# Whole sequences: logits ahead of their row transposes, and four scatters a pair

## The chip, the cores and the metric

The kernel runs on one core of a Trainium2 chip. A core has a matrix engine (TensorE, "PE" in the profile; its weight loads are "PEld"), a vector engine (VectorE, "DVE"), a scalar engine (ScalarE, "ACT"), GpSimd ("POOL") and a sync engine ("SP") that here only issues transfers. Each engine works through its own list of instructions in order; semaphores order the engines among each other. The metric is the device time of one execution in microseconds.

## The reference

A depthwise causal convolution over 7 positions, with softmaxed taps per head, feeds a mixture of experts with one expert per token. The expert of a token depends on the token before it: where the local gate is at least 0.5, the previous expert is kept.

```python
x = einsum('hk,bskhg->bshg', softmax(weight), windows_of_7(x))   # 8 x 3584 x 192
logits = x @ w_gate;  local = sigmoid(x @ w_local)               # 8 experts
for b in range(B):
    prev_e = -1
    for s in range(S):
        fresh_e = argmax(logits[b, s])
        e = fresh_e if s == 0 or local[b, s] < 0.5 else prev_e
        prev_e = e
        h = maximum(x[b, s] @ w1[e], 0)                          # 192 x 1024
        out[b, s] = softmax(logits[b, s])[e] * (h @ w2[e])       # 1024 x 192
```

## The kernel before

28672 tokens are worked through in 11 parts, numbered 0 to 10. Parts 0 to 5 are half sequences (1792 tokens; `SMALL` is 6). Parts 6 to 10 are whole sequences (3584 tokens, 28 tiles of 128). The diff speaks of the latter wherever it has `g >= SMALL`.

Each part from 2 on goes through these steps:

- **Convolution**, `conv` (L467). A part is held as six blocks of channels. For each, ScalarE writes the first tap into `z` (`firsts`, L481), and VectorE adds the other six (L499), so 36 steps of VectorE. There is one `z` for whole sequences, so the next part's first tap must wait until this part's `z` has been read. The loads of the following part's input (`load_chunk`, L180, on SP's queue) are issued between the steps.
- **Logits**, `logits` (L680). PE multiplies `z` with the gate weights (L707, 96 matmuls), ScalarE copies the result out of PSUM into `ls` (L712), VectorE transposes it (`lq`, L719), and sixteen small copies bring it into token order (`lt`; ScalarE at L733 for parts 6 to 9, VectorE at L735 otherwise). `rows_turned` (L687) transposes `z` into rows, one row a token, which later go to memory: four transposes of VectorE (L690). For whole sequences these four stand ahead of the logits, for half sequences behind the copies into `ls`.
- **Routing**, `route` (L741): argmax, the scan that carries the expert along, and a running count per expert give each token its place (`posi`, L888). The part's tiles are then appended to the list `to_put`.
- **Scatter**, `put` (L915). One call takes one tile of 128 tokens off `to_put` and issues on GpSimd's queue an indirect transfer of its rows to their places in `slots` (L922). With `behind`, it waits for a given matmul, so that the scatters are spread out in time.
- `tables` (L897) then fixes which expert each block of rows has.

Beside this runs the expert work, block by block, over rows that have been scattered already: 21 single blocks of 128 tokens, then pairs of 256 (blocks 21 to 58), then blocks of 512 from block 59 (`FIRST`) to 85, then pairs and singles. A pair is a hidden stage (`hidden`, L1142: 48 matmuls at L1153, four Relus of ScalarE at L1162), an output stage (`output`, L1165: 64 matmuls at L1177), and its way out: ScalarE scales one half (L1187), VectorE adds the other (L1191), GpSimd sends the rows to the output (`deliver`, L1205; the second of a pair is held back until the next hidden stage). A block of 512 takes `seven` (L1305, products at L1322, copies at L1328 to L1336) and `output_late` (L1360, matmuls at L1372). A block's rows are loaded on SP's queue (`load_rows`, L1082) and transposed by VectorE (L1134 for pairs); its expert's weights come at L1066, up to three blocks ahead. `ensure` (L1502) loads the rows of a block only once all scatters of its part have been issued.

What stands where on the engines is decided by a planner, `step` (L1432). It is called with a budget of VectorE time: for a pair 3.9 after the hidden stage, 1.2 after the output stage, ahead of L1191, and 3.3 at the end. It spends the budget on `conv` or `route`, whose `yield`s give the cost of what they just issued: 1.15 for a step of the convolution of a whole sequence, 0.24 times 7 tiles, 1.68, for each of the four row transposes. What is overspent is taken off the next budget. Three words are yielded beside costs:

- `"pe"` ends the route's turn; its logits are issued when the planner is called the next time (in blocks of 512, the next time at one place of a later block).
- `"hop"` lets the next part's convolution start, if it may (`st["turned"]`), and gives it the rest of the budget.
- `"placed"` does nothing.

The scatters of a pair are issued in `output`, behind the matmuls named in `spots`: at three places, or at five while more than 14 tiles wait (`len(to_put) > NT`). `spots` maps a place to the number of tiles that must be left in the list for it to be used.

Of the kernel before, what the change touches and what calls it, by code (L numbers as in the profile page):

```python
# [24 lines left out]
NT = 14  # L25
# [106 lines left out]
def kernel(  # L132
# [372 lines left out]
    def wide_route(g, y_sb, lt):  # L505
# [91 lines left out]
        nc.vector.tensor_copy(posi, pos)  # L597
        nc.vector.tensor_tensor(y[:, :, 0], pr, rs, op=Alu.mult)
        for b in range(NB):
            to_put.append((HALF if g and b < NH else g, y[:, b, :], posi[:, b:b + 1]))  # L600
        yield
        if g == 0:
            first_table(upto[:, :, NB], pos)
# [76 lines left out]
    def logits(g, z):  # L680

        nt = NTS[g]
        tq = (nt + 3) // 4
        y_sbs = row_tiles(g)
        zt = z.rearrange("p b (t s) -> p t b s", s=Q)

        def rows_turned():  # L687
            for t in range(0, nt, tq):
                u = min(t + tq, nt)
                nc.vector.transpose(y_sbs[t // NT][:, t % NT:t % NT + u - t, Y0:Y0 + D]  # L690
                                    .rearrange("p t (b s) -> p t b s", s=Q), zt[:, t:u])
                yield 0.24 * (u - t)

        if g >= SMALL:
            yield from rows_turned()
        yield "pe"
        if late_p or st["block"] >= TURNED:
            both = (st["bank"].tile([P, 2, 512], F32, name="ps") if late_p
                    else xps_p.tile([P, 2, 512], F32, name="xps"))
            lps = [both[:, half, :tq * Q] for half in range(2)]  # L700
        else:
            lps = [hps_p.tile([P, tq * Q], F32, name="hps") for half in range(2)]
        begin = [min(tq * j, nt - tq) for j in range(4)]
        for b in range(DQ):
            for j in range(4):
                for half, rows in halves():
                    nc.tensor.matmul(lps[half][Q * j:Q * j + Q, :], lhsT=wgq[rows, b, :],  # L707
                                     rhs=z[rows, b, begin[j] * Q:(begin[j] + tq) * Q],
                                     start=(b == 0), stop=(b == DQ - 1))
        ls = tmp(g, "ls", [P, 2, tq * Q], bufs=1)  # L710
        for half in range(2):
            nc.scalar.copy(ls[:, half, :], lps[half])  # L712
        if g < SMALL:
            yield from rows_turned()
        st["turned"] = g
        if g >= SMALL:
            yield "hop"
        lq = tmp(g, "lq", [P, 2 * tq, Q], bufs=1)
        nc.vector.transpose(lq.rearrange("p t e -> p (t e)"), ls.rearrange("p h x -> p (h x)"))  # L719
        yield 0.4  # L720
        lt = tmp(g, "lt", [P, nt, E + 1])
        aside = SMALL <= g < LAST
        if aside and late_p:
            yield "hop"
        for r in range(4):
            for j in range(4):
                t, u = tq * j, min(tq * (j + 1), nt)
                at = r // 2 * tq + t - begin[j]
                e0 = r % 2 * (E + 1)
                dst = lt[Q * r:Q * r + Q, t:u, :]  # L730
                src = lq[Q * j:Q * j + Q, at:at + u - t, e0:e0 + E + 1]
                if aside:
                    nc.scalar.copy(dst, src)  # L733
                else:
                    nc.vector.tensor_copy(dst, src)  # L735
                    yield 0.12
            if aside and r % 2:
                yield "hop"
        return y_sbs, lt

    def route(g):  # L741
# [145 lines left out]
        posi = sm.tile([P, nt], I32, name="posi", bufs=3)  # L887
        nc.vector.tensor_copy(posi, pos)  # L888
        for t in range(nt):
            to_put.append((g, y_sbs[t // NT][:, t % NT, :], posi[:, t:t + 1]))  # L890
        yield 0.2
        nc.vector.tensor_tensor(base, base, nps[:, 1, :E], op=Alu.add)
        yield 0.2
# [21 lines left out]
    def put(behind=None):  # L915


        if not to_put:
            return
        g, rows, to = to_put.pop(0)  # L920
        nc.gpsimd.nop()
        ins = nc.gpsimd.indirect_dma_start(  # L922
            out=slots[:, :], in_=rows, in_offset=None,
            out_offset=bass.IndirectOffsetOnAxis(ap=to, axis=0)).ins
        if behind is not None:
            tc.add_manual_dep(ins, behind.ins.name, SYNC, reason="scatters apart")
        if puts:
            tc.declare_no_dep(ins, group="puts", reason="slots of their own")
        if g:
            tc.declare_no_dep(ins, group="gets", reason="those slots were full before")  # L930
        puts.append((g, ins))
        tc.add_to_no_dep_group("puts", ins)
        tc.add_to_no_dep_group(f"puts{g}", ins)
# [73 lines left out]
    def fill(g):  # L1007


        lim = sm.tile([P, E], F32, name="lim")  # L1010
        nc.vector.tensor_scalar(lim, used, float(UT), None, Alu.mult)
        yield 0.2
        to = sm.tile([P, E], F32, name="to")
        nc.vector.tensor_scalar(to, base, i_of, None, Alu.add)
        yield 0.2
        over = sm.tile([P, E], F32, name="over")
        nc.vector.tensor_tensor(over, to, lim, op=Alu.is_ge)
        yield 0.2
        nc.vector.tensor_tensor(to, to, ec, op=Alu.add)
        yield 0.2  # L1020
        nc.vector.tensor_scalar(to, to, 1.0, None, Alu.add)
        yield 0.2
        far = sm.tile([P, E], F32, name="far")
        nc.vector.scalar_tensor_tensor(far, ef, float(UT), to, Alu.mult, Alu.subtract)
        yield 0.2
        nc.vector.tensor_scalar(far, far, float((DUMMY + 1) * UT), None, Alu.add)
        yield 0.2
        nc.vector.scalar_tensor_tensor(far, far, i_of, over, Alu.add, Alu.mult)
        yield 0.2
        nc.vector.tensor_tensor(to, to, far, op=Alu.add)  # L1030
        yield 0.2
        toi = sm.tile([P, E], I32, name="toi")
        nc.vector.tensor_copy(toi, to)
        yield 0.2
        for e in range(E):
            to_put.append((PADS, pad, toi[:, e:e + 1]))


    blocks = [(0, 1, i, next(g for g in FULL if i < FULL[g])) for i in range(ONE[-1])]
# [102 lines left out]
    def hidden(n, wb, xT, w1):  # L1142
# [4 lines left out]
        for two in range(2):  # L1147
            hps = [hps_p.tile([P, 2, BT], F32, name="hps") for half in range(2)]
            for d in range(KD):
                for j in range(2):  # L1150
                    f0 = (d * 4 + two * 2 + j) * P
                    for half, rows in halves():
                        ins = nc.tensor.matmul(hps[half][:, j, w], lhsT=wb[rows, w1 + f0:w1 + f0 + P],  # L1153
                                               rhs=xT[rows, d, w], start=(d == 0 and j == 0),
                                               stop=(d == KD - 1), skip_group_check=True)
                if two and d == 0 and held:
                    held.pop(0)(ins)
                if n == 1 and (two, d) == (0, 0) and st["block"] and not (st["hot"] or few()):
                    put(ins)
            for half in range(2):  # L1160
# [4 lines left out]
    def output(n, wb, xg, hT, w2):  # L1165
# [2 lines left out]
        away = st["due"] and not (to_put and to_put[0][0] == 3)  # L1168
        spots = {1: {(0, 0, 1): 0} if st["block"] and not away else {},
                 2: {(0, 0, 0): 0, (0, 1, 1): 2, (2, 0, 7): 0}}[n]  # L1170
        if to_put and (to_put[0][0] in (HALF, 3) or n > 1 and len(to_put) > NT):
            spots.update({1: {(2, 0, 3): 0}, 2: {(2, 0, 2): 0, (2, 1, 6): 0}}[n])
        for m4 in ([0, 1, 4, 5], [2, 3, 6, 7]):
            for k in range(n):
# [568 lines left out]
```

## Time and profile before

| | us |
|---|---|
| median of three runs | 1308.93 (1304.45 to 1313.44) |
| profiled execution | 1307.49 |
| its span, first to last instruction | 1305.6 |

The timeline lists an engine's instructions as start, duration, engine, line, operation, what it writes and reads, and how many of the same kind were merged (x2). What stands in brackets is how long the engine had been idle before it, and what ended that. "issue" means that nothing the profile shows was waited for. The ends of matmuls are modelled. The page gives, for each engine, its busy time, its share of the span, and the number of its instructions; the row "DMA" is the busy share of the transfer engines in 40 equal slices, in tenths; the chain is the work that ended last, followed back from the end.

Pairs run from about 180 us to 614 us of the span, blocks of 512 from there to about 1170 us.

### The profile page before, as it was taken

What the parts mean: (1) busy time and instruction counts of PE and PEld (TensorE: products, weight loads), DVE (VectorE), ACT (ScalarE), POOL (GpSimd) and SP (SyncE); (2) the same over time, 40 slices, a digit from 0 to 9 for tenths busy, and PEclk for the clock granted to TensorE, in tenths of its full rate; (3) what the DMA queues carried; (4) which work ended last, traced back from release to release, by engine and by line L of the source; (5) the groups of instructions that cost most, each with busy time, mean ns of one, the idle gap of its engine ahead of it and who ended that gap; (6) DMA issues with size and microseconds to landing.
All of it is one profiled execution on the core that took longest, in us unless ns stands there. A gap on an engine that the chain in (4) does not pass through costs nothing.

```text
span 1305.6 us, 37317 instructions
## 1 busy us (share of the span) xinstructions
PE 1265.1 (97%) x14674; PEld 1216.0 (93%) x14674; DVE 878.0 (67%) x1951; ACT 524.7 (40%) x1039; POOL 589.4 (45%) x636
## 2 busy tenths in 40 slices
PE   9899999999999999999999999999999999999997
PEld 8799989999988889889999998999999999999997
DVE  6889778989787787787869889578544435421111
ACT  5455533334243333424445444353434434432232
POOL 4544451536226446447633567435666433321111
PEclk9999999999999999999999999999999999999999
DMA  5899898959858869768755636274655544546794
GB/s 198 275 412 345 346 343 247 299 169 354 293 158 275 272 179 323 253 211 248 204 158 133 178 119 201 83 189 144 168 173 142 167 142 118 156 124 211 233 330 148
DMA packets 187784, 284.61 MB, mean 218 GB/s; under 512 B 150352, under 2 KB 160775, under 8 KB 174162
## 3 DMA queue, kind: packets, MB, share of 16 engines
q1 hardware_dynamic: 165280, 236.94, 57.8%
q0 software_dynamic: 22320, 45.22, 10.3%
q8 instruction: 117, 1.92, 0.6%
q14 instruction: 65, 0.53, 0.1%
q10 hardware_dynamic: 2, 0.00, 0.0%
HBM read 236.50 MB, written 46.07 MB: 216 GB/s over the span
## 4 chain that ended last, share of the span: by engine, by line
PE 89%; DVE 5%; issue 2%; DMA 1%; ACT 1%; POOL 0%; another core or an unknown queue 0%; SPq 0%; POOLq 0%; DVEq 0%; ACTq 0%
PE ps L1372 24%; PE yps L1177 20%; PE hps L1153 19%; PE ps L1322 14%; PE ps L1267 5%; PE xps L1322 3%; DVE arena L499 2%; DMA hT<-slots 1%; PE xps L707 1%; PE hps L281 1%; DMA wb<-in_w_dram 0%; PE ps L707 0%; DVE xT L1246 0%; PE hps L218 0%; DVE hot L662 0%
## 5 line engine op out<-in xcount | busy, mean ns | idle before, releaser
L1205 POOL DMA_INDIRECT out_dram<-o_sb,head x208 | 230.5, 1108 | 468.9 <-DVE o_sb L1387 289.7
L1372 PE MATMUL ps<-wb,hot 64*128 64x192 f32 x4224 | 354.0, 323 | 1.1 <-issue 0.7
L1372 PEld LDWEIGHTS ps<-wb,hot 64*128 64x128 f32 x4224 | 343.9, 187 | 6.6 <-issue 3.8
L499 DVE SCALAR_TENSOR_TENSOR arena<-arena,c 128x896 f32<-128x896 f32 (+1 forms) x324 | 305.2, 951 | 38.0 <-ACT arena L481 30.9
L922 POOL DMA_INDIRECT slots<-arena,posi x228 | 236.8, 1039 | 162.0 <-PE yps L1177 82.8
L1177 PE MATMUL yps<-wb,hT 64*128 64x192 f32 x3104 | 279.9, 331 | 11.7 <-ACT hT L1162 7.6
L1153 PE MATMUL hps<-xT,wb 64*128 64x256 f32 (+1 forms) x2832 | 279.7, 342 | 7.1 <-issue 6.5
L1177 PEld LDWEIGHTS yps<-wb,hT 64*128 64x128 f32 x3104 | 267.5, 192 | 17.7 <-ACT hT L1162 9.8
L1153 PEld LDWEIGHTS hps<-xT,wb 64*128 64x128 f32 x2832 | 250.3, 188 | 25.9 <-issue 13.0
L1162 ACT ACTIVATE hT<-hps 128x512 f32<-128x512 f32 (+1 forms) x236 | 110.1, 520 | 157.9 <-PE hps L1153 120.4
L1387 DVE SCALAR_TENSOR_TENSOR o_sb<-ps,head,o_sb 128x192 f32<-128x192 f32 x132 | 49.5, 412 | 155.3 <-ACT o_sb L1382 154.3
L1382 ACT ACTIVATE o_sb<-ps,head 128x192 f32<-128x192 f32 x132 | 49.1, 418 | 233.8 <-PE ps L1372 223.0
L1322 PE MATMUL ps<-xT,wb 64*128 64x256 f32 x864 | 104.2, 376 | 0.5 <-DVE xT L1298 0.5
L1322 PEld LDWEIGHTS ps<-xT,wb 64*128 64x128 f32 x864 | 91.8, 187 | 1.2 <-issue 0.9
L1187 ACT ACTIVATE o_sb<-yps,head 128x192 f32<-128x192 f32 x76 | 27.9, 418 | 152.5 <-PE yps L1177 127.5
L1343 DVE TENSOR_TENSOR hot<-xps,hot 128x512 f32<-128x512 f32 x54 | 37.0, 685 | 62.0 <-PE xps L1322 61.6
L1267 PE MATMUL ps<-xT,wb 64*128 64x128 f32 (+1 forms) x912 | 66.7, 299 | 0.0
L1267 PEld LDWEIGHTS ps<-xT,wb 64*128 64x128 f32 x912 | 65.1, 188 | 0.0
L1344 ACT ACTIVATE hot<-hot 128x512 f32<-128x512 f32 x54 | 34.1, 632 | 74.9 <-DVE hot L1343 62.7
L1322 PE MATMUL ps<-xg 64*128 64x256 f32 x432 | 58.0, 380 | 2.9 <-issue 1.0
L1191 DVE SCALAR_TENSOR_TENSOR o_sb<-yps,head,o_sb 128x192 f32<-128x192 f32 x76 | 28.1, 411 | 40.1 <-ACT o_sb L1187 24.8
L1246 DVE STREAM_TRANSPOSE xT<-arena 128x768 f32<-128x768 f32 (+1 forms) x37 | 31.7, 887 | 33.0 <-PE ps L1267 21.8
(308 smaller groups left out, 1340.3 us busy)
## 6 DMA issues: line engine op xcount, KB each, us to landing
wb<-in_w_dram SPq DMA_DIRECT2D x101, 1536.0 KB
arena<-in_xl_dram SPq DMA_DIRECT2D x30, 544.0 KB
hot<-slots SPq DMA_DIRECT2D x152, 96.0 KB
arena<-slots SPq DMA_DIRECT2D x56, 192.0 KB
hT<-slots SPq DMA_DIRECT2D x52, 192.0 KB
arena<-in_x_dram SPq DMA_DIRECT2D x4, 1920.0 KB
wb<-in_w_dram SPq DMA_DIRECT2D x12, 512.0 KB
slots<-arena,posi POOLq DMA_INDIRECT x228
```

Source lines behind the costliest of these rows:

```text
L499: nc.vector.scalar_tensor_tensor(z[:, b, :], chans(b, k), c[:, b, k:k + 1], z[:, b, :], Alu.mult, Alu.add)
L922: ins = nc.gpsimd.indirect_dma_start(out=slots[:, :], in_=rows, in_offset=None, out_offset=bass.IndirectOffsetOnAxis(ap=to, axis=0)).ins
L1153: ins = nc.tensor.matmul(hps[half][:, j, w], lhsT=wb[rows, w1 + f0:w1 + f0 + P], rhs=xT[rows, d, w], start=(d == 0 and j == 0), stop=(d == ...
L1162: nc.scalar.activation(hT[:, m:m + 2, w], hps[half][:, :, w], Act.Relu)
L1177: ins = nc.tensor.matmul(yps[half][:, k * D:(k + 1) * D], lhsT=hT[rows, m, k * P:(k + 1) * P], rhs=wb[rows, w2 + m * D:w2 + (m + 1) * D], ...
L1205: sent = nc.gpsimd.indirect_dma_start(out=out, in_=o, in_offset=None, out_offset=bass.IndirectOffsetOnAxis(ap=xg.bitcast(I32)[:, k, 1:2], ...
L1267: nc.tensor.matmul(hps[:, half, j, :], lhsT=wb[rows, f0:f0 + P], rhs=xT[rows, d, :], start=(d == 0 and j == 0), stop=(d == KD - 1), skip_g ...
L1322: ins = nc.tensor.matmul(to[:, half, j, :], lhsT=b[rows, j * P:(j + 1) * P], rhs=a[rows, :], start=(first and j == 0), stop=True, skip_gro ...
L1343: nc.vector.tensor_tensor(h11[:, side], wbk[:, side], h11[:, side], op=Alu.add)
L1372: ins = nc.tensor.matmul(yps[:, half, k * D:(k + 1) * D], lhsT=h[two][rows, side, j, k * P:(k + 1) * P], rhs=wb[rows, f * D:(f + 1) * D], ...
L1382: nc.scalar.activation(o_sb[:, k, :], yps[:, 0, k * D:(k + 1) * D], Act.Copy, scale=xg[:, at + k, 0:1])
L1387: nc.vector.scalar_tensor_tensor(o_sb[:, k, :], yps[:, 1, k * D:(k + 1) * D], xg[:, at + k, 0:1], o_sb[:, k, :], Alu.mult, Alu.add)
```

## The change

It does four things.

1. For parts 6 to 10, the row transposes are issued behind the logits and the copies into `ls`, as for the smaller parts. The `"hop"` behind them is gone.
2. Each entry of `to_put` also holds the number of the block in which its position was computed (-1 for the first two parts and for padding). A `put` that is tied to a matmul does nothing if the entry at the head of the list was computed in the current block. This holds until block 59; from there on the rule is off (`late_p` is set).
3. The pair's hidden stage gets a scatter, behind the second of the three groups of matmuls of its first half (`(two, d) == (0, 1)`), for parts 6 and up.
4. The two extra places in a pair's output stage are left to part 3 (and to the half part); the rule "more than 14 wait" is gone. So a pair has four scatters for whole sequences, and three for half sequences.

```diff
@@ wide_route, parts 0 and 1
-            to_put.append((HALF if g and b < NH else g, y[:, b, :], posi[:, b:b + 1]))
+            to_put.append((HALF if g and b < NH else g, y[:, b, :], posi[:, b:b + 1], -1))
@@ logits
-        if g >= SMALL:
-            yield from rows_turned()
         yield "pe"
...
         for half in range(2):
             nc.scalar.copy(ls[:, half, :], lps[half])
-        if g < SMALL:
-            yield from rows_turned()
+        yield from rows_turned()
         st["turned"] = g
-        if g >= SMALL:
-            yield "hop"
@@ route
-            to_put.append((g, y_sbs[t // NT][:, t % NT, :], posi[:, t:t + 1]))
+            to_put.append((g, y_sbs[t // NT][:, t % NT, :], posi[:, t:t + 1], st["block"]))
@@ put
-        if not to_put:
+        if not to_put or behind is not None and not late_p and to_put[0][3] == st["block"]:
             return
-        g, rows, to = to_put.pop(0)
+        g, rows, to, _ = to_put.pop(0)
@@ fill
-            to_put.append((PADS, pad, toi[:, e:e + 1]))
+            to_put.append((PADS, pad, toi[:, e:e + 1], -1))
@@ hidden
+                if n == 2 and (two, d) == (0, 1) and to_put and to_put[0][0] >= SMALL:
+                    put(ins)
@@ output
-        if to_put and (to_put[0][0] in (HALF, 3) or n > 1 and len(to_put) > NT):
+        if to_put and to_put[0][0] in (HALF, 3):
             spots.update({1: {(2, 0, 3): 0}, 2: {(2, 0, 2): 0, (2, 1, 6): 0}}[n])
```

## The prediction

> **What bounds the kernel now.** Read in this order: the page (busy shares, slices, chain), then the timeline of ScalarE cut to line 1187, then the timelines of the odd pairs.
>
> ```profile
> PE 1265.1 (97%) x14674; PEld 1216.0 (93%) x14674; DVE 878.0 (67%) x1951; ACT 524.7 (40%) x1039; POOL 589.4 (45%) x636
> ...
> DMA  5899898959858869768755636274655544546794
> ...
> PE 89%; DVE 5%; issue 2%; DMA 1%; ACT 1%; POOL 0%; another core or an unknown queue 0%; SPq 0%; POOLq 0%; DVEq 0%; ACTq 0%
> ```
>
> PE bounds it: 89% of the chain. A change to planning and scatters can only win the places where PE loses time, so I look for these. L1187 empties a pair's result as soon as PE has it, so the distance between two of its starts is what a pair took.
>
> ```profile
> 341.55 0.73 ACT L1187 ACTIVATE o_sb<-yps,head 128x192 f32<-128x192 f32 x2 [4.18 <-PE yps L1177]
> 351.93 0.73 ACT L1187 ACTIVATE o_sb<-yps,head 128x192 f32<-128x192 f32 x2 [4.18 <-PE yps L1177]
> 369.83 0.73 ACT L1187 ACTIVATE o_sb<-yps,head 128x192 f32<-128x192 f32 x2 [2.65 <-PE yps L1177]
> 380.21 0.73 ACT L1187 ACTIVATE o_sb<-yps,head 128x192 f32<-128x192 f32 x2 [3.84 <-PE yps L1177]
> ...
> 426.14 0.73 ACT L1187 ACTIVATE o_sb<-yps,head 128x192 f32<-128x192 f32 x2 [3.23 <-PE yps L1177]
> ...
> 446.90 0.73 ACT L1187 ACTIVATE o_sb<-yps,head 128x192 f32<-128x192 f32 x2 [4.11 <-PE yps L1177]
> 462.76 0.73 ACT L1187 ACTIVATE o_sb<-yps,head 128x192 f32<-128x192 f32 x2 [0.96 <-PE yps L1177]
> 473.14 0.73 ACT L1187 ACTIVATE o_sb<-yps,head 128x192 f32<-128x192 f32 x2 [3.84 <-PE yps L1177]
> ...
> 519.63 0.73 ACT L1187 ACTIVATE o_sb<-yps,head 128x192 f32<-128x192 f32 x2 [4.12 <-PE yps L1177]
> ...
> 540.39 0.73 ACT L1187 ACTIVATE o_sb<-yps,head 128x192 f32<-128x192 f32 x2 [4.12 <-issue]
> 557.95 0.73 ACT L1187 ACTIVATE o_sb<-yps,head 128x192 f32<-128x192 f32 x2 [2.65 <-PE yps L1177]
> ...
> 578.71 0.73 ACT L1187 ACTIVATE o_sb<-yps,head 128x192 f32<-128x192 f32 x2 [4.12 <-PE yps L1177]
> ...
> 614.55 0.73 ACT L1187 ACTIVATE o_sb<-yps,head 128x192 f32<-128x192 f32 x2 [4.11 <-PE yps L1177]
> ```
>
> These are the ends of blocks 35, 36, 37, 38, 42, 44, 45, 46, 50, 52, 53, 55 and 58. An undisturbed pair takes 351.93 - 341.55 = 10.38 us. Two sorts of places take longer. (a) The pairs ahead of which a whole sequence's logits run: 17.90, 15.86 and 17.56 us (parts 6, 7, 8). (b) The pairs just after a part's positions were computed: blocks 39 to 42 took 45.93 us, 4.41 over four pairs; 47 to 50 took 46.49, 4.97 over; 56 to 58 took 35.84, 4.70 over three. Together (b) is 14.1 us.
>
> Sort (a), from the timeline of part 6:
>
> ```profile
> 352.13 2.50 PE L707 MATMUL xps<-arena,wg 64*32 64x224 f32 x96
> 355.22 1.98 ACT L481 ACTIVATE arena<-arena,c 128x896 f32<-128x896 f32 x2
> 356.31 2.34 DVE L499 SCALAR_TENSOR_TENSOR arena<-arena,c 128x896 f32<-128x896 f32 x2 [8.29 <-ACT arena L481]
> 359.22 0.64 DVE L719 STREAM_TRANSPOSE arena<-arena 128x448 f32<-128x448 f32 x1
> 359.94 2.04 ACT L733 COPY arena<-arena 32x63 f32<-32x63 f32 x8 [2.74 <-DVE arena L719]
> 362.00 2.06 ACT L1162 ACTIVATE hT<-hps 128x512 f32<-128x512 f32 x4
> 362.65 7.15 PE L1177 MATMUL yps<-wb,hT 64*128 64x192 f32 x64 [2.64 <-ACT hT L1162]
> ...
> 457.26 4.98 PE L1177 MATMUL yps<-wb,hT 64*128 64x192 f32 x58 [2.58 <-ACT hT L1162]
> ```
>
> The logits cost PE 2.50 and that stays. But the eight copies of L733 stand on ScalarE ahead of the Relu L1162 that PE waits for; they wait for L719, which stands on VectorE behind L499, which waits for L481, which waits for the logits. VectorE sits idle 8.29 us and PE 2.64, and PE's next 64 matmuls then take 7.15, where half a pair, 5.19, is usual. So (a) is 17.90 - 12.88 = 5.02, 2.98 and 4.68: 12.7 us. After much the same gap, 2.58, part 7's matmuls did not slow (4.98 for 58), so the slow-down is a matter of chance. [...]
>
> **The change, part by part.** *Logits first.* The planner spends 3.9, 1.2 and 3.3 on a pair, 1.15 for a tap and four times 1.68 for the row transposes. In block 35 the 3.9 ends with the last tap of part 6; the 1.2 starts the route, which now says "pe" at once, and the 3.3 emits the logits. They move from the end of block 36 to the end of block 35, likewise 44 to 43, 52 to 51, and in the late blocks 61 to 60 and 69 to 68. The four transposes, L719 and the copies follow in block 36. Their rows:
>
> ```profile
> 340.16 1.58 DVE L690 STREAM_TRANSPOSE arena<-arena 128x1344 f32<-128x1344 f32 x1
> 342.66 3.03 DVE L690 STREAM_TRANSPOSE arena<-arena 128x1344 f32<-128x1344 f32 x2
> 345.61 0.94 DVE L1134 STREAM_TRANSPOSE xT<-hot 128x768 f32<-128x768 f32 x1
> ...
> 437.22 1.58 DVE L690 STREAM_TRANSPOSE arena<-arena 128x1344 f32<-128x1344 f32 x1
> ```
>
> From the end T of block 35's output (341.5) VectorE does L1191 to T+1.2, two transposes to 4.2, L1134 to 5.2, two more to 8.2, L719 to 8.9; ScalarE copies to 10.9 and runs the next part's two first taps (L481) to 12.9. PE has logits to 2.5, hidden stage to 7.7, output to 12.9. Both Relus of block 36 are ahead of the copies on ScalarE, and L1187 is due at 12.9, so nothing stands before PE; the second eight copies run from 13.6 to 15.7 while PE's next half hidden stage ends at 15.5. Gain: 12.7. Cover: if L1134 is late by over 2 us (its rows not landed), L1187 is late by the excess, and PE needs its banks at T+18.
>
> What is late next: z, the convolved part, itself. Formerly the transposes hid it. Part 6's z was ready at 340.16, before PE came (341.5). Part 7's was ready at 437.22, when block 43's output had ended 0.7 before (10.38 before 446.90, so 436.52). I charge 0.7 for parts 7 and 8 each, 1.4; the bounds are 0 and 1.4. Next taps start on VectorE some 3 us after L719, idle time that costs PE nothing. SP's chunk loads, issued with the taps, move half a block earlier past that pair's scatters only.
>
> *Late blocks.* Part 9's logits come a block earlier. Their old cost and the new one:
>
> ```profile
> 680.03 2.00 PE L1322 MATMUL ps<-xT,wb 64*128 64x256 f32 x16 [0.53 <-DVE xT L1298]
> ...
> 687.91 1.13 PE L1322 MATMUL ps<-xT,xg 64*128 64x256 f32 x8 [0.69 <-DVE hot L1346]
> ```
> ```profile
> 656.98 1.01 ACT L1328 COPY hot<-ps 128x1024 f32<-128x1024 f32 x1 [0.18 <-PE ps L1322]
> 658.38 1.09 PE L1322 MATMUL ps<-xg 64*128 64x256 f32 x8
> ```
>
> Old waits 0.53 + 0.69 = 1.2 go. New: eight copies (2.04) and one first tap (0.99) are emitted in block 61's last step, ahead of L1328 of block 62, which PE needs 0.39 after its end: 2.04 + 0.99 - 0.39 = 2.6 lost (0 if the banks hide it; 4.6 with a slow stretch of 1.95 behind it). Part 10's copies are VectorE's and stay hidden.
>
> *Scatters.* Positions come half a block earlier (end of 38 for 39, and so on). 28 scatters go four a pair, one of them in the hidden stage, where there were five and then three. POOL gains no work: at 1.27 us apart, four and two deliveries take 7.6 of 10.38. The new one stands ahead of the held delivery; that result buffer is wanted two blocks on. Part 5's scatters start a block later, so SP loads block 38's rows with block 39's; weights queued behind them are wanted three blocks on. Sort (b), from block 39:
>
> ```profile
> 387.93 0.18 DVE L888 CAST posi<-pos 128x28 int32<-128x28 f32 x1
> ...
> 388.88 0.97 POOL L922 DMA_INDIRECT slots<-arena,posi  x1 [3.98 <-PE yps L1177]
> ...
> 391.68 0.35 SPq L1066 DMA_DIRECT2D wb<-in_w_dram  x1
> ...
> 393.96 1.83 POOL L922 DMA_INDIRECT slots<-arena,posi  x1 [0.30 <-issue]
> ...
> 395.32 0.49 PE L1153 MATMUL hps<-xT,wb 64*128 64x256 f32 x2 [0.26 <-issue]
> ```
> ```profile
> 278.49 0.73 ACT L1187 ACTIVATE o_sb<-yps,head 128x192 f32<-128x192 f32 x2 [3.93 <-PE yps L1177]
> ...
> 300.03 0.73 ACT L1187 ACTIVATE o_sb<-yps,head 128x192 f32<-128x192 f32 x2 [3.25 <-issue]
> ```
>
> The positions come after the matmuls behind which the block's scatters were put, so five go out back to back, with the next weights (391.68) beside them, and PE falters in the next hidden stage for no releaser shown. Part 5, with three scatters in such a run, lost only 300.03 - 278.49 - 20.76 = 0.78. The new run: positions came 387.93 - 380.21 = 7.7 into block 39 and now come a 3.3 step earlier, at about 4.5; the four scatters and the held delivery behind them take 6.4 and end at 10.9, ahead of the next weights (391.68 - 380.21 = 11.5). No row shows such a run, so the gain lies between nothing (below it, see the rival) and 14.1; I take part 5's 0.78 for each of the three as nearest: 14.1 - 2.3 = 11.8 won, and 0.8 at part 5, whose run goes.
>
> Sum against the profiled execution's 1307.49 (span 1305.6, 1.9 around it): -12.7 +1.4 -1.2 +2.6 -11.8 -0.8 = -22.5, so 1285.0. The median of the runs shown, 1308.93, is 1.4 higher: **1286.5**.
>
> **The rivals.** *The faltering stays:* it comes from the weights and chunks, which keep their place, not from the scatters. For it: no releaser is shown. Against: it follows each such run and no ordinary pair. Then 1286.5 + 11.8 = **1298**. [...]
>
> *It only moves:* if VectorE is some 3 us later than counted, PE waits as long for z, or for banks behind a late L1187, as it did for the Relu, and the scatters meet the weights after all. Then 12.7 and 11.8 are not won, the 1.4 being part of it: 1286.5 + 24.5 - 1.4 = **1310**. Against: the slack counted above.
>
> *Slower:* the scatter in the hidden stage makes PE falter there, in each of the 20 pairs that get one (39 to 58). At 0.78 each that is 15.6 over 1298, **1314**; from 1.2 us each it is over 1% slower (1322). For it: all faltering was in a hidden stage. Against: pairs with three spaced scatters ran at 10.38.
>
> **How the numbers follow.** A measurement of this kernel tells about 1% from no change, 13 us. Forecast 0.56, faltering stays 0.25, moves 0.11, slower 0.08. Faster: 0.54 of the first and 0.03 of the second, 0.57; slower 0.08; within 1% the rest, 0.35. The range reaches from all of 14.1 won, no wait for z and no loss at block 62 (1286.5 - 2.3 - 1.4 - 2.6 = 1280, less a us of scatter) to the second case with slow stretches behind two new gaps (1298 + 3.9, 1302); likeliest case alone: 1279 to 1292.
>
> **What would show it.** Right: L1187 distances of 12.9 to 13.6 where the logits run, no idle 8.29 on VectorE, L733 ended before L1187 is due; 10.38 to 10.6 in the pairs after the positions; a wait of L1322 on ScalarE at block 62's start. Wrong: PE waiting on L499 at L707, matmuls with "issue" gaps in hidden stages, or SP's row loads landing after L1134 wants them.

## The result and the profile after

The changed kernel took 1288.55 us, the median of four runs (1286.63 to 1289.84), beside 1309.97 for the kernel before on the same chips. The ratio is 0.9839, with a 95% interval of 0.9801 to 0.9877: 1.6% faster. The prediction was 1286.5 (1279 to 1302). The profiled execution took 1289.84, its span is 1288.0.

Of the page of the changed kernel: busy time of the engines and shares of the chain of waits.

```profile
PE 1255.7 (97%) x14674; PEld 1207.1 (94%) x14674; DVE 879.3 (68%) x1951; ACT 523.8 (41%) x1039; POOL 593.6 (46%) x636
...
PE 93%; DVE 4%; issue 1%; ACT 1%; POOL 0%; another core or an unknown queue 0%; POOLq 0%; DVEq 0%; ACTq 0%
```

PE still bounds the kernel, with more of the chain (93% after 89%) and less "issue" (1% after 2%). The work is the same, the losses are fewer. Lines of the changed kernel carry smaller numbers: L1187 is now L1184, L707 is L705, L1177 is L1174, L733 is L728, L922 is L917, L1191 is L1188, L1205 is L1202, L1298 is L1295, L1322 is L1319, L1328 is L1325.

The timeline of ScalarE cut to L1184, the end of each pair's output. The rows are those of blocks 35, 36, 38, 42, 43, 44, 51, 52 and 58.

```profile
343.65 0.73 ACT L1184 ACTIVATE o_sb<-yps,head 128x192 f32<-128x192 f32 x2 [4.12 <-PE yps L1174]
357.65 0.73 ACT L1184 ACTIVATE o_sb<-yps,head 128x192 f32<-128x192 f32 x2 [0.21 <-PE yps L1174]
...
378.41 0.73 ACT L1184 ACTIVATE o_sb<-yps,head 128x192 f32<-128x192 f32 x2 [4.12 <-PE yps L1174]
...
419.93 0.73 ACT L1184 ACTIVATE o_sb<-yps,head 128x192 f32<-128x192 f32 x2 [4.12 <-PE yps L1174]
430.31 0.73 ACT L1184 ACTIVATE o_sb<-yps,head 128x192 f32<-128x192 f32 x2 [4.12 <-issue]
444.33 0.73 ACT L1184 ACTIVATE o_sb<-yps,head 128x192 f32<-128x192 f32 x2 [0.22 <-PE yps L1174]
...
516.99 0.73 ACT L1184 ACTIVATE o_sb<-yps,head 128x192 f32<-128x192 f32 x2 [4.12 <-issue]
531.05 0.73 ACT L1184 ACTIVATE o_sb<-yps,head 128x192 f32<-128x192 f32 x2 [0.22 <-PE yps L1174]
...
593.54 0.73 ACT L1184 ACTIVATE o_sb<-yps,head 128x192 f32<-128x192 f32 x2 [4.28 <-PE yps L1174]
```

The pairs with logits are now 36, 44 and 52, and take 14.00, 14.02 and 14.06 us instead of 17.90, 15.86 and 17.56. Blocks 39 to 42 take 419.93 - 378.41 = 41.52, four times the undisturbed 10.38: PE no longer falters behind the positions. From the end of block 35 to that of block 58 stand 23 pairs and three logits, 23 x 10.38 + 3 x 2.50 = 246.2 us without a loss. The kernel before took 614.55 - 341.55 = 273.0 there, the new one 593.54 - 343.65 = 249.9. So it lost 26.8 us in this stretch and now loses 3.7. This number, the **loss of the stretch**, is used for all kernels below. The rest of the 3.7 beside the logits is 0.2, in blocks 53 and 58.

The timeline around the logits of part 6:

```profile
343.55 1.99 PEld L705 LDWEIGHTS xps<-arena,wg 64*32 64x32 f32 x78 [0.23 <-issue]
343.55 3.49 PE L705 MATMUL xps<-arena,wg 64*32 64x224 f32 x96
...
344.77 3.03 DVE L690 STREAM_TRANSPOSE arena<-arena 128x1344 f32<-128x1344 f32 x2
344.80 0.98 POOL L1202 DMA_INDIRECT out_dram<-o_sb,head  x1 [1.23 <-DVE o_sb L1188]
...
346.10 0.51 PEld L705 LDWEIGHTS xps<-arena,wg 64*32 64x32 f32 x18 [0.56 <-issue]
...
353.42 2.01 ACT L728 COPY arena<-arena 32x63 f32<-32x63 f32 x8
355.46 1.98 ACT L481 ACTIVATE arena<-arena,c 128x896 f32<-128x896 f32 x2
...
356.54 2.34 DVE L499 SCALAR_TENSOR_TENSOR arena<-arena,c 128x896 f32<-128x896 f32 x2 [4.44 <-ACT arena L481]
```

The logits start on time, with nothing from L499 to wait for. The copies L728 and the two first taps L481 end at 357.44, just ahead of L1184 at 357.65. But the logits themselves take 3.49 us, where they took 2.50, with a gap of 0.56 in their weight loads. That is about 1.0 in each of three parts, most of what is left of the 3.7.

### The profile page after: what moved, and what is told of

Read it like the earlier page. It is cut to its first block, busy times and chain, and to the rows that moved or that the text cites. A ratio compares the mean times of both kernels' runs of the same rounds, so it can differ in the third digit from the quotient of the medians.

```text
span 1288.0 us, 37312 instructions
## 1 busy us (share of the span) xinstructions
PE 1255.7 (97%) x14674; PEld 1207.1 (94%) x14674; DVE 879.3 (68%) x1951; ACT 523.8 (41%) x1039; POOL 593.6 (46%) x636
## 4 chain that ended last, share of the span: by engine, by line
PE 93%; DVE 4%; issue 1%; ACT 1%; POOL 0%; another core or an unknown queue 0%; POOLq 0%; DVEq 0%; ACTq 0%
PE ps L1369 25%; PE hps L1148 20%; PE yps L1174 20%; PE ps L1319 16%; PE ps L1264 5%; PE xps L1319 3%; PE xps L705 1%; DVE arena L499 1%; PE hps L281 1%; PE ps L705 1%; PE hps L218 0%; DVE hot L662 0%; PE hps L705 0%; PE yps L668 0%
## 5 line engine op out<-in xcount | busy, mean ns | idle before, releaser
L1202 POOL DMA_INDIRECT out_dram<-o_sb,head x208 | 220.9, 1062 | 458.3 <-DVE o_sb L1384 298.5
L499 DVE SCALAR_TENSOR_TENSOR arena<-arena,c 128x896 f32<-128x896 f32 (+1 forms) x324 | 305.1, 951 | 24.9 <-ACT arena L481 17.6
L917 POOL DMA_INDIRECT slots<-arena,posi x228 | 251.8, 1104 | 145.7 <-PE yps L1174 66.0
L1148 PE MATMUL hps<-xT,wb 64*128 64x256 f32 (+1 forms) x2832 | 273.3, 341 | 4.2 <-issue 3.9
L1174 PE MATMUL yps<-wb,hT 64*128 64x192 f32 x3104 | 273.3, 326 | 3.2 <-ACT hT L1159 2.5
L1174 PEld LDWEIGHTS yps<-wb,hT 64*128 64x128 f32 x3104 | 261.2, 188 | 7.5 <-ACT hT L1159 3.7
L1148 PEld LDWEIGHTS hps<-xT,wb 64*128 64x128 f32 x2832 | 246.4, 188 | 21.5 <-issue 8.1
L1319 PE MATMUL ps<-xT,wb 64*128 64x256 f32 x864 | 104.5, 376 | 2.6 <-DVE xT L1295 2.6
L1319 PEld LDWEIGHTS ps<-xT,wb 64*128 64x128 f32 x864 | 91.6, 187 | 3.8 <-issue 3.4
L1184 ACT ACTIVATE o_sb<-yps,head 128x192 f32<-128x192 f32 x76 | 27.8, 417 | 128.3 <-PE yps L1174 105.1
L1319 PE MATMUL ps<-xg 64*128 64x256 f32 x432 | 57.7, 380 | 6.5 <-POOL xg L1285 3.0
L1319 PEld LDWEIGHTS ps<-xg 64*128 64x128 f32 x432 | 45.3, 187 | 9.9 <-POOL xg L1285 3.7
```

Source lines behind the costliest of these rows:

```text
L499: nc.vector.scalar_tensor_tensor(z[:, b, :], chans(b, k), c[:, b, k:k + 1], z[:, b, :], Alu.mult, Alu.add)
L917: ins = nc.gpsimd.indirect_dma_start(out=slots[:, :], in_=rows, in_offset=None, out_offset=bass.IndirectOffsetOnAxis(ap=to, axis=0)).ins
L1174: ins = nc.tensor.matmul(yps[half][:, k * D:(k + 1) * D], lhsT=hT[rows, m, k * P:(k + 1) * P], rhs=wb[rows, w2 + m * D:w2 + (m + 1) * D], ...
L1202: sent = nc.gpsimd.indirect_dma_start(out=out, in_=o, in_offset=None, out_offset=bass.IndirectOffsetOnAxis(ap=xg.bitcast(I32)[:, k, 1:2], ...
L1319: ins = nc.tensor.matmul(to[:, half, j, :], lhsT=b[rows, j * P:(j + 1) * P], rhs=a[rows, :], start=(first and j == 0), stop=True, skip_gro ...
```

## The experiments

All are judged by the ratio to the kernel before on the same chip, and by the loss of the stretch in their own profiles (last row of block 58 less that of block 35, less 246.2).

| kernel | ratio, 95% interval | loss of the stretch, us |
|---|---|---|
| before | 1 | 26.8 |
| whole change | 0.9839 (0.9801 to 0.9877) | 3.7 |
| whole change, again (c1) | 0.985 (0.9829 to 0.9871) | 3.5 |
| e1 part 1 alone | 0.983 (0.9808 to 0.9851) | 6.5 |
| e2 parts 2 to 4 | 0.9905 (0.9884 to 0.9926) | 13.9 |
| e3 part 2 alone | 0.9958 (0.9934 to 0.9983) | 19.0 |
| e4 other order of products | 0.9815 (0.9794 to 0.9837) | 3.6 |
| e5 delivery held back | 0.9815 (0.9791 to 0.9838) | 1.3 |
| e5b the same, again | 0.9812 (0.9787 to 0.9838) | 1.3 |
| e6 run of four, output stage | 0.9888 (0.9862 to 0.9913) | 8.4 |
| e7 run of four, hidden stage | 0.9977 (0.996 to 0.9995) | 23.3 |
| e8 the same with pauses | 0.9883 (0.9851 to 0.9916) | 13.2 |
| e9 e5 and late blocks | 0.9807 (0.9777 to 0.9836) | 1.3 |
| e10 e1 with delivery held back | 0.9835 (0.9805 to 0.9865) | 5.4 |

The loss of the stretch comes from one profile a row, but it repeats: 3.7 and 3.5 for the whole change, 1.3 and 1.3 for e5.

### Which part did it

**e1**, the kernel before with part 1 alone:

```diff
-        if g >= SMALL:
-            yield from rows_turned()
         yield "pe"
...
-        if g < SMALL:
-            yield from rows_turned()
+        yield from rows_turned()
         st["turned"] = g
-        if g >= SMALL:
-            yield "hop"
```

> Part 1 of the change alone: logits ahead of the row transposes; the scatters by the old rule (five a pair while more than 14 wait, no block left out). The positions then come at the end of block 38, so the five scatters of block 39 find them there and go out spread over the output stage. Theory R (PE falters only behind a run of scatters that goes out back to back because the positions came late): both sorts of loss go, 10.38 us in the pairs after the positions, about 1289 us, as with the whole change. Theory D (five scatters a pair beside the weight loads are the cause, however they are spread): blocks 39 to 42, 47 to 50 and 56 to 58 still take some 14 us more than their 10.38 each, about 1302 us.

Measured: 0.983, the same as the whole change within the interval; loss 6.5. The timeline of ScalarE of this kernel, the ends of blocks 38 and 43:

```profile
378.62 0.73 ACT L1182 ACTIVATE o_sb<-yps,head 128x192 f32<-128x192 f32 x2 [4.11 <-PE yps L1172]
...
431.00 0.73 ACT L1182 ACTIVATE o_sb<-yps,head 128x192 f32<-128x192 f32 x2 [4.15 <-issue]
```

Five scatters a pair are still issued, but these five pairs take 431.00 - 378.62 = 52.4 us, 0.5 over; the three places together lost 2.8 instead of 14.1. The part that moves the logits also removed most of the faltering: the positions came half a block earlier, so the scatters found them ready and went out where they were put. Theory D, by which five scatters a pair lose some 14 us however they are spread, fell.

**e2**, the changed kernel with part 1 undone (the reverse of the diff above):

> Parts 2 to 4 alone: four scatters a pair, none in the block in which its position was computed; logits behind the row transposes as before. The pairs with logits still take 17.9, 15.9 and 17.6 us, the late blocks their old time. Theory R: the late positions of block 39 start no run, the scatters begin spread in block 40, no faltering: 1310 - 14 = 1296 us. Rival (the faltering went because the positions came half a block earlier): it stays, 1308 to 1310 us.

Measured: 0.9905. The pairs with logits took 15.91, 15.86 and 18.31, in all 50.1 where the kernel before took 51.3. That is 11.4 over, so of the loss of 13.9 the faltering behind the positions has 2.5 us, where it had 14.1: nearly as far as theory R had it. The rival, by which it goes only with earlier positions, fell.

**e3**, the kernel before with the rule of part 2 alone:

```diff
...
-        if not to_put:
+        if not to_put or behind is not None and not late_p and to_put[0][3] == st["block"]:
             return
...
```

> Part 2 alone: no scatter in the block in which its position was computed; otherwise as before, five a pair. Theory R: no run, faltering gone, 1296 us. Theory D (five a pair): it stays, 1308 to 1310 us. The pairs with logits as before, 17.9, 15.9 and 17.6 us.

Neither: 0.9958, and a loss behind the positions of 8.3 us instead of 14.1. The run behind block 39 is gone, but a new one formed behind block 41 (four scatters and a delivery, 1.26 apart, from 411.85 on), since five a pair stand close together in the output stage. So theory R has to be put in terms of spacing, not of late positions.

**e10**, part 1 with the delivery held back (the edit of e5 below), beside e5b, which has parts 2 to 4 as well:

> Part 1 of the change with the delivery held back, without parts 2 to 4. In the run of part 1 alone the pairs behind the positions lost 2.8 us against 0.2 with the whole change. If parts 2 to 4 are worth that, this is 2.6 us above the control, 0.9835 of the kernel before; if they are worth nothing, the same as the control.

0.9835 beside 0.9812: the intervals overlap, so the runs don't tell them apart. The traces do: a loss of 5.4 beside 1.3, and 6.5 (e1) beside 3.6 (e4) without the held delivery. Parts 2 to 4 are worth 3 to 4 us, 0.3%, once part 1 is in.

### What makes PE falter

**e6 and e7** put the four scatters of a pair at one place:

```diff
-                if n == 2 and (two, d) == (0, 1) and to_put and to_put[0][0] >= SMALL:
-                    put(ins)
...
+        run = n == 2 and to_put and to_put[0][0] >= SMALL
+        if run:
+            spots = {(0, 0, 0): 0}
...
-                        put(ins)
+                        for _ in range(4 if run else 1):
+                            put(ins)
```

> The whole change, but the four scatters of a pair for whole sequences are issued at one place, behind the first matmuls of the output stage, one right after the other; none in the hidden stage. Their number and blocks are the same. At that place the loads that SP issued at the pair's start have mostly landed. Theory R (a run of scatters is enough): the 20 pairs that carry them lose PE time, at part 5's 0.78 each some 16 us. Theory RD (it takes a run beside the loads of weights, rows and chunks): about the time of the whole change, within 4 us.

e7 has the same loop, in the hidden stage, and no spots in the output stage:

> The whole change, but the four scatters of a pair for whole sequences are issued at one place, behind the second group of matmuls of the hidden stage, one right after the other; none in the output stage. There SP's loads of weights, rows and chunks are under way. Theory R and theory RD: the 20 pairs lose PE time, 0.78 to 4.7 each, 16 to 90 us in all. Rival (runs do not matter, only that the positions were late): the time of the whole change.

e6 lost 8.4 (4.7 more than the change), e7 lost 23.3. So neither place is free, as the rival to theories R and RD had it; but the 16 us that theory R put for e6 did not come either. The two don't tell the place from the length of a run: in e6 GpSimd often idled some 2 us behind the four scatters, while in blocks 39 and 47 of e7 they stood in runs of six. The timelines of GpSimd and of PE's weight loads in block 39 of e7:

```profile
380.99 0.99 POOL L1205 DMA_INDIRECT out_dram<-o_sb,head  x1 [7.34 <-DVE o_sb L1191]
382.28 0.97 POOL L917 DMA_INDIRECT slots<-arena,posi  x1 [0.30 <-issue]
383.56 0.96 POOL L917 DMA_INDIRECT slots<-arena,posi  x1 [0.31 <-issue]
384.82 0.96 POOL L917 DMA_INDIRECT slots<-arena,posi  x1 [0.30 <-issue]
386.08 0.96 POOL L917 DMA_INDIRECT slots<-arena,posi  x1 [0.30 <-issue]
386.70 0.21 PEld L1177 LDWEIGHTS yps<-wb,hT 64*128 64x128 f32 x2 [0.72 <-issue]
387.35 1.80 POOL L1205 DMA_INDIRECT out_dram<-o_sb,head  x1 [0.30 <-issue]
388.12 0.20 PEld L1177 LDWEIGHTS yps<-wb,hT 64*128 64x128 f32 x2 [1.21 <-issue]
```

Six transfers start 1.27 us apart. Five microseconds after the first, PE's weight loads stop for 0.72 us, go on for two loads, and stop for 1.21, and pair 39 takes 14.98. In pair 40 of the same kernel as many scatters stand at the same place, and it takes 10.38:

```profile
395.27 3.53 DVE L499 SCALAR_TENSOR_TENSOR arena<-arena,c 128x896 f32<-128x896 f32 x3
395.31 0.99 POOL L1205 DMA_INDIRECT out_dram<-o_sb,head  x1 [6.16 <-DVE o_sb L1191]
396.60 1.86 POOL L917 DMA_INDIRECT slots<-arena,posi  x1 [0.30 <-issue]
398.76 0.96 POOL L917 DMA_INDIRECT slots<-arena,posi  x1 [0.30 <-issue]
398.93 5.41 PEld L1177 LDWEIGHTS yps<-wb,hT 64*128 64x128 f32 x64
399.62 4.56 DVE L499 SCALAR_TENSOR_TENSOR arena<-arena,c 128x896 f32<-128x896 f32 x4
400.03 1.53 POOL L917 DMA_INDIRECT slots<-arena,posi  x1 [0.30 <-issue]
401.87 0.96 POOL L917 DMA_INDIRECT slots<-arena,posi  x1 [0.30 <-issue]
403.13 1.90 POOL L1205 DMA_INDIRECT out_dram<-o_sb,head  x1 [0.30 <-issue]
```

Here half of the transfers take 1.5 to 1.9 us, beside taps of VectorE (L499), the starts lie 1.3 to 2.2 apart (1.56 in the mean), and the 64 weight loads run through. The pairs of the kernel before (180 to 614 us) show the same: of 52 transfers with no tap beside them the longest took 1.02 us, while of 129 with one 37 took over 1.3 and up to 1.91. Not every transfer beside a tap is long: those at 395.31 and 401.87 took 0.99 and 0.96. Why some are is not shown. Behind the positions VectorE fixes the tables, in steps of at most 0.34 us beside one transpose of 0.98, and the first five transfers of block 39 took 0.96 to 0.99 there; this fits the place of the loss.

**e8** puts a short work of GpSimd behind each scatter of e7:

```diff
                     for _ in range(4):
                         put(ins)
+                        nc.gpsimd.memset(sm.tile([P, 256], F32, name="pause", bufs=1), 0.0)
```

> The run of four scatters in the hidden stage once more, with a memset of GpSimd (128 x 256) behind each of them, so that the transfers are issued some 1.6 us apart or more instead of 1.27. Their number, their place and the loads beside them are the same. In the run without pauses the pairs 39, 47, 53 and 55 lost 4.6, 4.4, 3.6 and 2.3 us; in 39 and 47 six transfers went out 1.27 apart; in pairs 40 to 42 the same scatters went out 1.6 to 2.2 apart, slowed by VectorE's taps, and PE lost 0 to 0.2. Theory RR (the spacing decides): pairs 39 and 47 lose less than 1 us each, the whole is some 12 us below the run without pauses, about 0.988 of the kernel before. Rival (the number of transfers beside the loads decides): no change, 0.998 of the kernel before.

The timeline of GpSimd in block 39 of this kernel:

```profile
382.07 0.97 POOL L917 DMA_INDIRECT slots<-arena,posi  x1 [0.30 <-issue]
383.03 0.33 POOL L1156 MEMSET pause<- 128x256 f32 x1
383.54 0.97 POOL L917 DMA_INDIRECT slots<-arena,posi  x1 [0.17 <-issue]
```

The pause gave a spacing of 1.46 instead of 1.27, less than was meant. Pair 39 took 12.62 instead of 14.98, pair 47 11.91 instead of 14.78. Theory RR had asked for a loss under 1 us in each; they lost 2.2 and 1.5. The whole is 0.9883 beside 0.9977, with intervals apart: the 12 us that were expected. The rival, no change, fell. A fifth of a microsecond more between transfers halves the loss of these pairs, with the number of transfers, their place and the loads unchanged. Outside the pairs with logits the loss of the stretch went from 18.5 to 6.8. In two pairs with logits it grew (44 and 52: 15.38 and 15.67 beside 14.52 and 14.87), for a reason given in the next section. That the spacing of GpSimd's transfers counts is shown; that nothing else contributes is not.

### What keeps the logits at 3.5 us

**c1** is the changed kernel again, as a control.

> The whole change once more, as the control for the three others of this set on the same chip: 0.984 times the kernel before.

**e4** begins the products with the block of channels that VectorE finishes last, so that PE's wait for it moves from the 41st of 48 pairs of products to the first:

```diff
-        for b in range(DQ):
+        for n, b in enumerate([DQ - 1] + list(range(DQ - 1)) if g >= SMALL else range(DQ)):
...
-                                     start=(b == 0), stop=(b == DQ - 1))
+                                     start=(n == 0), stop=(n == DQ - 1))
```

> The whole change, with the gate products of whole sequences starting at the last block of channels, the one that is convolved last; the sum over the blocks is taken in another order. In the changed kernel PE waits for VectorE at the 41st of 48 pairs of products, and L705 takes 3.4 us where it took 2.5. Theory W (the wait in the middle, though met, makes the gap of 0.56 and the rest): with the wait at the first product L705 takes 2.5 again in parts 6 to 8, 3 x 0.9 less, about 1286 us. Rival (the gap comes from elsewhere, as it does in parts 9 and 10, which have no such wait): L705 stays at 3.4, 1288.5 us.

The pairs took 14.03, 14.02 and 14.05, the gap stayed: theory W fell. What all logits with a gap had in common was a transfer that GpSimd issued beside them. So it was in the kernel before, where part 10's logits alone took 3.44 us instead of 2.50 (timeline of the kernel before):

```profile
841.25 1.26 POOL L1205 DMA_INDIRECT out_dram<-o_sb,head  x1 [4.82 <-DVE o_sb L1387]
...
842.53 0.17 PEld L707 LDWEIGHTS ps<-arena,wg 64*32 64x32 f32 x5 [0.56 <-issue]
```

**e5** (and e5b, the same on another chip) holds that delivery back:

```diff
-                if two and d == 0 and held:
+                if two and d == 0 and held or not two and d == 2 and len(held) > 1:
                     held.pop(0)(ins)
...
-            if k == 0 and not st["hot"]:
+            if k == 0 and not st["hot"] and not (n > 1 and st["due"] and st["block"] >= TURNED):
                 deliver(o_sb[:, 0, :], xg, 0)
```

> The whole change; in the pairs behind which logits are issued, the delivery that follows L1188 at once is held back as well, until the third group of matmuls of the next hidden stage. So no transfer of GpSimd is issued beside the gate products. In the runs so far each of eight logits beside which such a transfer was issued had a gap of about 0.56 in its weight loads and took 3.4 us, and each of nine without one had no gap and took 2.5 us. Theory P (the transfer that GpSimd issues makes the gap): L705 takes 2.5 us in parts 6 to 8, the three pairs 13.1 instead of 14.0, 2.8 us less than the whole change. Rival Q (the row transposes of VectorE that now run beside the products make it): L705 stays at 3.4 us, no change.

> The version that holds the delivery back while logits run, once more as the control for the next two on the same chip: 0.9815 of the kernel before.

The timeline of e5 around part 7's logits:

```profile
430.19 2.07 PEld L705 LDWEIGHTS xps<-arena,wg 64*32 64x32 f32 x96 [0.23 <-issue]
...
431.40 3.03 DVE L690 STREAM_TRANSPOSE arena<-arena 128x1344 f32<-128x1344 f32 x2
...
436.16 0.99 POOL L1202 DMA_INDIRECT out_dram<-o_sb,head  x1 [0.30 <-issue]
```

All 96 weight loads run through in 2.07, in parts 6, 7 and 8 alike, with the row transposes still beside them. Theory P holds, rival Q falls. All 14 profiles agree, by number too: of their 70 logits of whole sequences, the 25 with no such transfer beside them took 2.50 or 2.51, the 41 with one 3.2 to 3.6 (beside the 3.60 of e1's part 8 a second one ended 0.1 us into them), and the 4 with two 4.3 to 4.4 (parts 7 and 8 of e6 and e8; this is why pairs 44 and 52 of e8 grew). Nor does the amount of data moved decide it: in the kernel before, part 6 had no gap while the transfer engines moved 207 GB/s (352.1 to 354.6 us), and part 10 had one at 18 GB/s (839.7 to 843.2). The median was 1287.36 (1283.0 to 1289.12) beside 1290.92 (1289.8 to 1292.45) for the control on the same chip, 3.6 less; the loss of the stretch fell from 3.5 to 1.3.

### The late blocks

**e9** adds two edits to e5: while late logits run, their block's first delivery is held back too, and the second eight copies of part 9 are issued one place later.

```diff
+                due = st["due"]
                 step(SIDE[2 + part], late_p[0] if part == 0 else None)
+                due = due and not st["due"]
...
-                if k == 0 or n < KQ:
+                if (k == 0 or n < KQ) and not (n == KQ and due):
...
-            if n == KQ and part and two == 0 and k and held:
+            if n == KQ and part and two == 0 and held and (k or len(held) > 1):
                 held.pop(0)(ins)
...
             if aside and r % 2:
                 yield "hop"
+                if late_p and r == 1:
+                    yield "hop"
```

> The same, and two edits in the late blocks: the delivery is held back there too while logits run, and the second eight copies of part 9's logits are issued one place later, so that L1325 of block 62 does not stand behind them. Expected: no gap of 0.56 in the logits of parts 9 and 10 (2 x 0.9), and L1325 of block 62 free of the copies' 2.0, with PE's wait of 1.11 gone: 2.9 us less than the control, 0.979 of the kernel before. Rival (the copies only delay L1341 and VectorE's first steps of the routing instead): 1.8 less or nothing.

The timeline of e9 (its L1327 is L1325 of the changed kernel):

```profile
630.61 2.07 PEld L705 LDWEIGHTS ps<-arena,wg 64*32 64x32 f32 x96 [0.23 <-issue]
...
660.21 1.01 ACT L1327 COPY hot<-ps 128x1024 f32<-128x1024 f32 x1
...
664.43 2.02 ACT L728 COPY arena<-arena 32x63 f32<-32x63 f32 x8
```

The gap in part 9's logits is gone (part 10's too), the copies stand behind L1327 instead of ahead of it, and PE's wait of 1.11 in block 62 is gone with them. The wait of 0.91 ahead of it stayed. From the end of block 58 to L1327 of block 64 it took 107.2 us, where e5b took 109.0. The median was 1288.49 beside 1291.09, 2.6 less, with ratios of 0.9807 and 0.9812: what the traces show, though the runs alone don't separate the two.

## Why the prediction was right

Both mechanisms held, and most of the time came where it was forecast. That the sum came so close is in part luck: the logits won 2.1 us less than forecast and the faltering 2.1 more, and the late blocks and the start of the span each cost 2 to 3 us that the sum did not have.

**The logits (forecast: 12.7 won, 1.4 lost to z).** The three pairs took 51.32 before and 42.08 after: 9.2 were won. The mechanism was right: no Relu waited for the copies any more, and VectorE's idle 8.29 is down to 4.44. The 1.4 did not come: VectorE's last tap of part 7 ended at 428.9, 1.3 before PE started the logits at 430.2. In its place came about 1.0 for each of three logits, 3.49 instead of 2.50 in part 6, which the prediction had carried over unchanged ("that stays"). It had counted the delivery of L1202 among GpSimd's work only, not as something that slows PE. Before, no transfer stood beside these logits.

**The slow clock.** The prediction counted the row of 7.15, behind a gap of 2.64, as a slow stretch and a matter of chance. The granted clock bears this out: it was 0.50 there from 365 to 367 us. The changed kernel has no gap of 2.6 there, but e3 has them. The timeline of its PE, parts 6 and 7:

```profile
366.33 5.47 PE L1177 MATMUL yps<-wb,hT 64*128 64x192 f32 x64 [2.64 <-ACT hT L1162]
```
```profile
457.38 7.15 PE L1177 MATMUL yps<-wb,hT 64*128 64x192 f32 x64 [2.58 <-ACT hT L1162]
```

After much the same gap the same matmuls run at full pace once (granted clock 1.00 from 367 to 372 us) and slowly once (0.50 from 458 to 460), so the slow stretch was rightly counted, and as a matter of chance.

**The faltering (forecast: 11.8 of 14.1 won).** All but 0.2 was won. The step that carried it, that no long run goes out back to back behind the positions, was right; the residue of 0.78 for each part was taken from part 5 and was too much. The short run that the prediction priced, ending ahead of the next weights, did not form: the positions came 1.8 us into block 39 instead of 4.5, so the block's scatters went out at their own places (381.51, 384.96, 386.23 and 388.14). The next weights were no danger either: they were issued at 388.83, amid transfers, and the pairs took 10.38. What the prediction had not seen is that transfers cost PE by their spacing, as e7 and e8 show (pair 39 took 14.98 at 1.27 us and 12.62 at 1.46), and that the spacing differs with what VectorE does beside it (0.96 to 0.99 us a transfer behind the positions, 1.5 to 1.9 beside some taps). The rival that the weights and chunks alone were the cause fell: they kept their place, and 1298 did not come. Nor did the amount of data moved slow PE there: pairs 39 to 42 of the changed kernel took 10.38 each at 293 to 337 GB/s. Beside the logits it was a transfer that GpSimd issued, and not the amount of data, that cost time (3.44 us at 18 GB/s with one, 2.50 at 207 without).

**Part 5 (0.8 won).** Blocks 30 and 31 take 10.38 each: 0.8 won.

**The late blocks (forecast: 1.4 lost).** From the end of block 58 to L1325 of block 64 it takes 110.1 us, where it took 106.6: 3.5 lost. The timeline of the changed kernel:

```profile
617.15 2.00 PE L1319 MATMUL ps<-xT,wb 64*128 64x256 f32 x16 [1.72 <-DVE xT L1295]
...
661.11 2.02 ACT L728 COPY arena<-arena 32x63 f32<-32x63 f32 x8
...
662.08 2.00 PE L1319 MATMUL ps<-xT,wb 64*128 64x256 f32 x16 [0.91 <-DVE xT L1295]
...
663.15 1.04 ACT L481 ACTIVATE arena<-arena,c 128x896 f32<-128x896 f32 x1
664.10 0.99 ACT L1325 COPY hot<-ps 128x1024 f32<-128x1024 f32 x1
...
665.19 1.13 PE L1319 MATMUL ps<-xg 64*128 64x256 f32 x8 [1.11 <-issue]
```

The copies and the first tap stand ahead of L1325, as forecast; PE's waits there are 0.91 + 1.11 = 2.0, where 2.6 was put. Only the 1.11 is the copies', as e9 shows: with them moved, the 0.91 stayed. Not foreseen were 1.0 for part 9's logits, again beside a delivery, and 1.72 in block 60, where L1295 came late behind six taps. The last is 1.72 in both profiles of the changed kernel, but e4 and e5b, which differ little up to there, have none. Whether it belongs to the change stays open.

**The rest.** By the end of block 32 the changed kernel's profile was 2.1 us behind that of the kernel before (312.51 beside 310.41), with part 5's 0.8 won in it: 2.9 lost ahead of that, where the two kernels hardly differ. The other profiles, much alike up to there, lie between 310.8 and 315.8, so this looks like spread; with one profile of the kernel before, the quickest there of all, it isn't shown. Behind block 64 the two differ by 0.1. The sum: -9.2 - 13.9 - 0.8 + 3.5 + 2.9 - 0.1 = -17.6, the 1305.6 - 1288.0 of the spans. The medians lie further apart, 21.4: the profiled execution was 2.5 us under the median of the kernel before, and 1.3 over that of the changed one.

**The rivals.** "It only moves" fell, since nothing waited for z. "Slower" fell too: the pairs with one scatter in their hidden stage run at 10.38. But its mechanism is real, and the margin is not wide: with four transfers at one place of the hidden stage instead of one, e7 gave nearly everything back (0.9977).

## What to carry to other kernels

In this kernel transfers that GpSimd issues had a price on PE. Six in a run, 1.27 us from start to start, cost a pair 4.4 to 4.6 us, at 1.46 they still cost 1.5 to 2.2, and at 1.56 in the mean nothing; beside the logits, 96 matmuls in 2.50 us, a single one cost 0.7 to 1.1. So try them further apart, and none beside a stretch in which PE has only very short matmuls. When an engine stops with "issue" as the only cause, look at what the other queues were issuing in the same microseconds, and compare stretches with and without it. And do one part at a time: the part that reordered the logits brought most of what the scatter rules were written for.

## What the runs showed of the hardware

In the kernels before and after, six of the ten logits of whole sequences had an indirect transfer of GpSimd beside them (0.98 to 1.26 us), and in each of the six PE's weight loads stopped for 0.56 to 0.61 us around its end. In the usual matmuls this can't be seen: pairs 39 to 42 of the changed kernel, with four spaced scatters and two deliveries each, took 10.38. In the logits, at 26 ns a product (2.50 us for 96), it shows at once. In e7's run at 1.27 us the weight loads of the usual matmuls stopped too, for 0.72 and 1.21 us, after four transfers. Why only then is not shown. What it is in the issue of a transfer that holds PE up stays open. Packets of the profile's instruction queue don't go with the gap: one fell into part 9's logits before (670.7 to 673.3 us), which had no gap, and none into part 7's after (430.2 to 433.8), which had one.

The granted clock fell behind short stops too. The windows of the kernel before in block 40 (stretch, its length, busy time of PE, weight loads, VectorE, ScalarE, GpSimd, then clock, DMA share and GB/s):

```profile
399.00:401.00 2.00, 2.00 (x16) 2.00 (x16) 1.93 (x3) 1.61 (x3) 1.41 (x1) 0.50 1.07 335
401.00:403.00 2.00, 2.00 (x24) 2.00 (x24) 0.50 (x1) 0.00 (x0) 0.77 (x2) 0.85 0.66 172
```

Ahead of this the weight loads had four gaps of 0.42 to 1.17 us (from 394.9 us on). Then the granted clock was 0.50, and PE did 16 matmuls in two microseconds and 24 in the next two, where 64 in 5.19 us, 25 in two, are usual. Part of the 4.4 us that blocks 39 to 42 lost is this; that the gaps caused it is not shown.
